# Filler constant first, no GpSimd copies, pad rows by DMA, and new engine lists in a fused attention and gated-MLP kernel

## The chip, the cores and the metric

The kernel runs on one core of a Trainium2 chip. A core has a matrix engine (TensorE, PE in the profile; PEld is its weight load), a vector engine (VectorE, DVE), a scalar engine with lookup tables (ScalarE, ACT), a general engine (GpSimd, POOL) and SyncE (SP), which here only issues DMAs. The engines run their own instruction streams in order and wait for one another through semaphores. Tensors live in SBUF (128 partitions); matmul results go to PSUM (eight banks), from which DVE or ACT must carry them away before a bank is used again. The metric is device time in microseconds, the median of several runs.

## What is computed

One layer with two halves, 2048 tokens, width 448, bfloat16. First a local attention: 16 heads of width 28, each token attends to itself and seven earlier tokens at a distance of 2, 4, ... 14. Then a gated MLP whose gate mixes all tokens with a 2048x2048 matrix.

```python
def A(x):                       # x is layernorm(input)
    qkv = x @ wqkv              # 448 -> 3 x 16 heads x 28
    idx = pos[:, None] - 2 * arange(8)[None, :]
    logits = einsum('bhsd,bhswd->bhsw', q, k[idx]) * 28 ** -0.5
    attn = softmax(where(idx >= 0, logits, -1e9))
    return einsum('bhsw,bhswd->bhsd', attn, v[idx]) @ wo
def B(x):                       # x is layernorm(h)
    z = gelu(x @ w_in)          # 448 -> 1792
    z1, z2 = z[..., :896], layernorm(z[..., 896:])
    g = einsum('ts,bsf->btf', w_sp, z2) + b_sp
    return (z1 * g) @ w_out     # 896 -> 448
h = x + A(layernorm(x)); out = h + B(layernorm(h))
```

## The kernel before

The kernel builds some 660 tasks, each a few instructions on one engine, and replays them in the order of five lists (`SEQ`: SP, POOL, DVE, ACT, PE, in that order), written out as task numbers. A planner class replays the lists with a cost for each task; this decides which PSUM banks and ring buffers a task gets, and how many filler matmuls go into a gap of PE. `Sched.issue` puts in the semaphore waits that the data needs. On the chip each engine then runs its list in order. `XV_ON` and the `alts` of a task say which engines may do it; the list in which its number stands decides.

The tokens are kept as 16 blocks of 128; unit u is the pair of blocks u and u+8. The work goes through these stages:

- Loads: x (`ld_x`, on SP and ACT), the q, k and v parts of `wqkv` (`ld_w` through `ld_rows`, lines 545 to 558, four DMAs each: two of 384 rows, two of 64 rows, alternating between the SP and ACT queues).
- First layernorm, unit by unit (`ln_unit`, line 616): statistics on DVE (line 622), aggregation on DVE (627), the reciprocal root on POOL (613, 614) or ACT (638, 639), normalization on DVE (646) into a ring, then a transpose into `xh`. Units 0 to 2 are transposed by PE and copied from PSUM (copies of every sort are on lines 608 and 610); units 3 to 7 by a DMA transpose on SP (653).
- The q and k weights are copied into a padded form, 32 columns to a head (`cpq`, `cpk`, on DVE or ACT), after GpSimd has zeroed the pads (593).
- q and k projections (line 764) in three chunks of tokens; two of 256 or 270 columns for each of k and q before the one of 512. The last chunk needs units 4 to 7.
- Nine attention tiles of 114 tokens. For each: a strided copy of `xh` into `xv` (`xv`, line 802; all nine on POOL), the v projection (812) and its evacuation (`evv`), logits (843), exp (857), a band mask on DVE (865), row sums (878), ln and exp for the reciprocal (887, 912), the product with v (901), and the scaling into `oT` (920).
- The output projection (958) and the residual sum on DVE (967) for each unit, then the second layernorm. The output weights `wo2` hold two heads in partitions 0 to 27 and 32 to 59; GpSimd first zeroes partitions 0 to 63 (`c_wo0`, line 597), two DMAs of 28x8 rows fill them, and `cpwo` (POOL) copies partitions 0 to 63 to 64 to 127.
- The MLP: `w_in` matmuls (979 and 1022) with gelu on ACT (989, 1032), a layernorm of z2 (995 to 1009), the token mixing (1056) from transposed loads of `w_sp` (939), gating on DVE (1066, 1073), the last projection (1082), the sum and the stores. The `w_sp` loads are chained: each waits until the one before it has landed.

PE, ACT and DVE share the four pairs of PSUM banks, so an evacuation that comes late holds a later matmul. The filler (`fill`, line 600) issues matmuls of 512 columns from a tile of ones, `warm`, which the task `c_warm` writes on DVE (line 586); the planner puts fillers only into gaps that begin after that task. In the list of before `c_warm` stands behind most of the first layernorm, and the built program holds no filler. The planner's price for a matmul does not depend on how long PE has been busy.

Of the kernel before, what the change touches and what calls it, by code (L numbers as in the profile page):

```python
# [6 lines left out]
D = 448  # L7
DH = 28
FH = 896
# [6 lines left out]
NC7 = 7  # L16
# [13 lines left out]
F32 = mybir.dt.float32  # L30
# [11 lines left out]
XV_ON = ("dve", "act", "pool")  # L42
# [184 lines left out]
class Planner:  # L227
# [64 lines left out]
    def replay(self, t0=0.7):  # L292
# [13 lines left out]
        for _ in tasks:  # L306
# [32 lines left out]
            dur = t.occ  # L339
            if e == "pe":  # L340
                live = [(f, s) for s, f in enumerate(self.pools["ps"]) if f is not None]
                if live and self.filler[0].end is not None:
                    tf, bank = min(live)
                    at = max(free[k], tf + 0.3, self.filler[0].end + 0.1)
                    if now - at > self.FILL[0]:
                        if pe_first is None:
                            pe_first = at
# [802 lines left out]
```

## Time and profile before

| | us |
|---|---|
| median of 3 runs | 252.19 (252.17 to 253.67) |
| the profiled execution | 250.46 |
| its span, first to last instruction | 248.7 |

The profile is of one execution. "Busy" counts instructions at work, without the issuing of DMAs; a DMA issue is shown on its queue (SPq, ACTq). The span in 40 slices of 6.2 us, the busy share of each in tenths:

```profile
PE   0699979969988999999999999999999999999995
DVE  4897725677999899078880002329010281553453
ACT  2639984667997556575850000000000000000000
POOL 6161630510083023014250000000000000000000
```

The first 13 or 14 slices are the attention and the start of the MLP, with work for all four engines; from the 14th on PE is full to the end. A row of the timeline gives start, duration, engine, line, operation, output and inputs with their shape, the count, and in brackets the idle time ahead of it with what ended it; rows of one kind that follow each other are merged, and the duration is that of the merged group. A row of the chain gives start, duration and what it was. A row of a group gives the count, the busy us, the mean ns of one, and the idle time ahead of it.

### The profile page before, as it was taken

The numbers are of one execution on the slowest core, as the hardware profiler recorded it, in microseconds if no ns is written. First come the engines' busy times: TensorE is split into PE (matmuls) and PEld (weight loads), VectorE is DVE, ScalarE is ACT, GpSimd is POOL, SyncE is SP. The second block draws the span as 40 slices with busy tenths as digits, with TensorE's granted clock in tenths as the row PEclk, the third lists the DMA queues.
The fourth block names the chain that finished last, engine by engine and source line by source line (L and its number), as shares of the span: only waits on it lengthen the run. The fifth ranks groups of instructions, "written<-read, shape, count | busy, mean of one in ns | idle before, by whom it ended". The sixth has DMA issues, their size and how long they took to land.

```text
span 248.7 us, 6335 instructions
## 1 busy us (share of the span) xinstructions
PE 231.4 (93%) x2822; PEld 121.3 (49%) x2822; DVE 136.4 (55%) x280; ACT 88.1 (35%) x104; POOL 40.7 (16%) x77
## 2 busy tenths in 40 slices
PE   0699979969988999999999999999999999999995
PEld 0476746445553555555544444444444444444552
DVE  4897725677999899078880002329010281553453
ACT  2639984667997556575850000000000000000000
POOL 6161630510083023014250000000000000000000
PEclk9999999999999999999999999999999999999999
DMA  6953698695349575677556333000000000000123
GB/s 184 349 154 64 165 148 191 124 179 106 44 26 206 101 194 60 133 161 134 130 87 168 85 87 84 0 0 0 3 0 0 0 3 0 0 0 18 58 101 122
DMA packets 56759, 22.81 MB, mean 92 GB/s; under 512 B 46668, under 2 KB 56604, under 8 KB 56732
## 3 DMA queue, kind: packets, MB, share of 16 engines
q1 hardware_dynamic: 55004, 20.98, 39.9%
q10 hardware_dynamic: 1728, 1.43, 1.8%
q8 instruction: 22, 0.36, 0.6%
q14 instruction: 5, 0.04, 0.0%
HBM read 9.20 MB, written 1.84 MB: 44 GB/s over the span
## 4 chain that ended last, share of the span: by engine, by line
PE 79%; DVE 11%; ACT 3%; DMA 2%; POOL 2%; ACTq 1%; issue 1%; DVEq 0%; POOLq 0%
PE psum L1056 39%; PE psum L979 9%; PE psum L1082 9%; PE psum L1022 9%; PE psum L764 7%; PE psum L958 4%; DVE reg L865 3%; DMA z2p<-in_A_wqkv_dram 2%; ACT reg L608 2%; DVE tring L646 2%; PE psum L812 2%; DVE st L622 2%; DVE x_tm L967 1%; DVE reg L610 1%; POOL rs L614 1%; PE psum L901 1%
## 5 line engine op out<-in xcount | busy, mean ns | idle before, releaser
L1066 DVE TENSOR_TENSOR reg<-psum,reg 128x512 bf16<-128x512 f32 x28 | 18.9, 687 | 69.9 <-PE psum L1056 69.8
L1056 PE MATMUL psum<-reg,z2p 128*128 128x512 bf16 x224 | 49.0, 379 | 0.0
L1056 PE MATMUL psum<-wspT_lo,z2p 128*128 128x512 bf16 x224 | 48.8, 379 | 0.0
L1056 PEld LDWEIGHTS psum<-wspT_lo,z2p 128*128 128x128 bf16 x224 | 21.9, 98 | 26.6 <-DVE z2p L1009 0.4
L1056 PEld LDWEIGHTS psum<-reg,z2p 128*128 128x128 bf16 x224 | 21.9, 98 | 26.3
L764 PE MATMUL psum<-xh,reg 64*128 64x256 bf16 (+2 forms) x336 | 28.9, 330 | 3.0 <-ACT reg L912 1.8
L608 ACT ACTIVATE reg<-psum 128x1024 bf16<-128x1024 f32 (+2 forms) x23 | 20.5, 917 | 9.9 <-PE psum L764 8.5
L764 PEld LDWEIGHTS psum<-xh,reg 64*128 64x128 bf16 x336 | 17.3, 103 | 12.4 <-ACT reg L608 2.2
L979 PE MATMUL psum<-w_in,xh 64*128 64x448 bf16 x224 | 22.6, 349 | 0.0
L1022 PE MATMUL psum<-xh,w_in 64*128 64x512 bf16 x196 | 22.2, 376 | 0.0
L995 DVE BATCH_NORM_STATS2 st<-z2p 128x6 f32<-128x448 bf16 x32 | 17.7, 608 | 8.2 <-ACT z2p L989 8.2
L1082 PE MATMUL psum<-reg 128*128 128x448 bf16 x112 | 21.7, 352 | 0.0
L622 DVE BATCH_NORM_STATS2 st<-x_tm 128x6 f32<-128x448 bf16 x32 | 18.9, 610 | 0.6 <-DMA x_tm<-in_A_x_dram 0.4
L989 ACT ACTIVATE z2p<-psum 128x896 bf16<-128x896 f32 x16 | 14.2, 917 | 8.7 <-PE psum L979 8.7
L1032 ACT ACTIVATE reg<-psum 128x1024 bf16<-128x1024 f32 x14 | 13.6, 1026 | 10.4 <-PE psum L1022 10.4
L857 ACT ACTIVATE reg<-psum 128x928 bf16<-128x928 f32 x18 | 16.1, 942 | 2.5 <-PE psum L843 2.5
L979 PEld LDWEIGHTS psum<-w_in,xh 64*128 64x128 bf16 x224 | 12.4, 94 | 9.3 <-issue 1.0
L614 POOL TENSOR_TENSOR rs<-rs,nhalf 128x2 f32<-128x2 f32 x19 | 16.1, 846 | 1.6
L1082 PEld LDWEIGHTS psum<-reg 128*128 128x128 bf16 x112 | 11.0, 98 | 10.4
L1022 PEld LDWEIGHTS psum<-xh,w_in 64*128 64x128 bf16 x196 | 11.0, 94 | 9.9 <-ACT reg L1032 0.5
L646 DVE TENSOR_SCALAR tring<-x_tm,mv,rs 128x448 bf16<-128x448 bf16 x32 | 14.6, 486 | 2.0 <-POOL rs L614 1.7
L865 DVE TENSOR_TENSOR reg<-reg,mband 128x928 bf16<-128x928 bf16 x18 | 13.5, 775 | 3.8 <-ACT reg L857 3.8
(63 smaller groups left out, 185.8 us busy)
## 6 DMA issues: line engine op xcount, KB each, us to landing
w_in<-in_B_w_in_dram SPq DMA_DIRECT2D x4, 672.0 KB, 5.3
out_dram<-tring SPq DMA_DIRECT2D x16, 112.0 KB, 1.7
x_tm<-in_A_x_dram SPq DMA_DIRECT2D x6, 224.0 KB, 6.0
reg<-in_B_w_out_dram SPq DMA_DIRECT2D x1, 784.0 KB, 4.5
z2p<-in_A_wqkv_dram ACTq DMA_DIRECT2D x2, 336.0 KB, 5.1
z2p<-in_A_wqkv_dram SPq DMA_DIRECT2D x2, 336.0 KB, 5.4
reg<-in_B_b_sp_dram SPq DMA_DIRECT2D x1, 512.0 KB, 4.1
w_in<-in_B_w_in_dram SPq DMA_DIRECT2D x4, 112.0 KB, 3.3
```

The lines of the kernel that those rows point to most:

```text
L608: iss("act", lambda e: e.activation(dst, src, AF.Copy), reads=rd, writes=wr)
L614: iss("pool", lambda e: e.tensor_tensor(dst, dst, nh, ALU.pow), reads=rr + [r_nhalf], writes=rr)
L622: iss("dve", lambda e: e.bn_stats(st[:, b, :], x_tm[:, b, :]), reads=[r_x[b]], writes=[rl[b]])
L646: iss("dve", lambda e: e.tensor_scalar(tring[:, h[0], :].rearrange("p (c s q f) -> p s q c f", c=NC7, s=2, q=2)[:, n], x_tm[:, b, :].rearr ...
L764: iss("pe", lambda e, k=k, s=s, gi=gi, lhs=lhs: e.matmul(psum[:, bk[s] * 512 + cw * gi:bk[s] * 512 + cw * gi + cw], lhs, xh[64 * s:64 * s ...
L865: iss(tk[0].eng, lambda e: e.tensor_tensor(ev, ev, mk, ALU.mult), reads=[r_E[es[0]][n], r_mband], writes=[r_E[es[0]][n]])
L979: iss("pe", lambda e, c=c, s=s: e.matmul(psum[:, zb[s] * 512:zb[s] * 512 + D], xh[64 * s:64 * s + 64, ROWS[s][c], HX + 128 * u:HX + 128 * ...
L995: iss("dve", lambda e, b=b: e.bn_stats(st3[:, b, k, :], z2p[:, b, D * k:D * k + D]), reads=[r_z2[b][k]], writes=[r_st3[b][k]])
L1022: iss("pe", lambda e, c=c, s=s: e.matmul(psum[:, bk[s] * 512:bk[s] * 512 + 512], w_in[64 * s:64 * s + 64, c, 128 * f:128 * f + 128], xh[64 ...
L1056: iss("pe", lambda e, b=b: e.matmul(psum[:, gb[0] * 512:gb[0] * 512 + 512], z2p[:, b, 128 * f:128 * f + 128], src[:, b, 512 * (tc % 2):512 ...
L1066: iss("dve", lambda e: e.tensor_tensor(ub[:, us_[0], :], psum[:, gb[0] * 512:gb[0] * 512 + 512], bb[:, 512 * tc:512 * tc + 512], ALU.add), ...
L1082: iss("pe", lambda e, f=f: e.matmul(psum[:, wb[0] * 512:wb[0] * 512 + D], z1p[f][:, 128 * m:128 * m + 128], w_out[:, f, :], start=(f == 0) ...
```

## The change

The diff does six things.

1. `c_warm` becomes the first task on DVE. All first statistics are made dependent on it, so that the lists keep it there.
2. `XV_ON` loses "pool", and `cpwo` stands on DVE: no copy is left on GpSimd.
3. The pads of the output weights are loaded instead of zeroed. `c_wo0` is gone. Each group of 28 rows is loaded as 32 rows, the next head's first four rows in the pad; the last group of the second half takes its pad from four earlier rows. (The matching rows of `oT` are zero, since V's pads are zero.) Four DMAs take the place of two.
4. The 64-row pieces of the q and k weights are loaded together: two DMAs of 64x2 rows for both in place of four. `ld_rows` is split into `rows384` and `rows64`.
5. In the planner, `COLD` takes the place of a fixed first stretch: after 1.8 us without a matmul, PE work counts up to 4.5 us as running at half speed.
6. All five lists are new. The first projections come later or earlier among the attention tiles, evacuations change between DVE and ACT, reciprocal roots between ACT and POOL.

```diff
-XV_ON = ("dve", "act", "pool")
+XV_ON = ("dve", "act")
...
-    FILL = (0.5, 0.25, 0.427, 0.216, 3.4)
+    FILL = (0.5, 0.25, 0.427, 0.216)
+    COLD = (1.8, 4.5)
...
+                if now - pe_end > self.COLD[0]:
+                    pe_run = now
+                cold = max(0.0, pe_run + self.COLD[1] - now)
+                dur += min(dur, 0.5 * cold)
                 dur += self.fetch(t.nmm, now, dur, True)
+                pe_end = now + dur
...
+        w_qk = z2flat[:, 0:2 * NC7 * D].rearrange("p (w c n) -> p w c n", w=2, c=NC7)
+        w_ld = {p: w_qk[:, n] for n, p in enumerate("qk")}
...
+        r_ld["k"][2:] = r_ld["q"][2:]
...
+        def rows384(name, dst, src, res, engs):
+            nb = 384 * src.shape[1] * 2
+            return [dma(engs[n], "%s%d" % (name, n), lambda e, d=d, f=f: e.dma_start(d, f.rearrange("(k p) n -> p k n", p=128)), nb,
+                        writes=[res[n]], issue=0.6) for n, (d, f) in enumerate(((dst[:, 0:3, :], src[0:384, :]), (dst[:, 3:6, :], src[64:448, :])))]
+
+        def rows64(name, dst, src, res, engs):
+            nb = 64 * src.shape[1] * 2
+            return [dma(engs[n], "%s%d" % (name, 2 + n), lambda e, d=d, f=f: e.dma_start(d, f), nb, writes=[res[2 + n]], issue=0.5, bw=180.0)
+                    for n, (d, f) in enumerate(((dst[0:64], src[384:448, :]), (dst[64:128], src[0:64, :])))]
...
-        c_wo0 = cst("c_wo0", [(lambda e: e.memset(reg3[0:64, 0:8 * D].bitcast(F32), 0.0), [], r_wo[0:2])], 1.55)
...
-                tb.append(add("bn%d_%d" % (which, b), "dve", 0.53, em, deps=[src_deps[n]]))
+                tb.append(add("bn%d_%d" % (which, b), "dve", 0.53, em, deps=[src_deps[n]] + ([c_warm] if which == 1 else [])))
...
-        for e_ in range(2):
-            t_wo.append(dma("sp", "wo%d" % e_, lambda e, e_=e_: e.dma_start(
-                wo2[32 * e_:32 * e_ + DH, :, :], A_wo.rearrange("(g h d) n -> h d g n", g=8, h=2)[e_]), DH * 8 * D * 2,
-                writes=[r_wo[e_]], deps=[c_wo0], bw=160.0))
+        for n, (dst, src) in enumerate((
+                (wo2[0:32], bass.AP(A_wo.tensor, A_wo.offset, [[D, 32], [2 * DH * D, 8], [1, D]])),
+                (wo2[32:64, 0:7], bass.AP(A_wo.tensor, A_wo.offset + DH * D, [[D, 32], [2 * DH * D, 7], [1, D]])),
+                (wo2[32:32 + DH, 7], A_wo[15 * DH:16 * DH, :]),
+                (wo2[32 + DH:64, 7], A_wo[15 * DH - 4:15 * DH, :]))):
+            t_wo.append(dma("sp", "wo%d" % n, lambda e, d=dst, f=src: e.dma_start(d, f), (256, 224, 28, 4)[n] * D * 2,
+                            writes=[r_wo[n]], bw=160.0))
...
-        tk.append(add("cpwo", "pool", 3.6, lambda: copy(tk[0].eng, wo2[64:128], wo2[0:64], r_wo[0:2], [r_wo[2]]), deps=t_wo,
-                      alts={"pool": 3.6, "dve": 1.10, "act": 3.15}))
+        tk.append(add("cpwo", "dve", 1.0, lambda: copy(tk[0].eng, wo2[64:128], wo2[0:64], r_wo[0:4], [r_wo[4]]), deps=t_wo,
+                      alts={"dve": 1.0, "act": 3.1}))
```

What the lists say around the start and the attention, by task names. `xv` number i belongs to tile i, `evv` is the evacuation of v, `evq` and `evk` those of q and k, `nrm` and `bn` belong to the layernorm, `cp` are weight copies, `ot` scales the product with v, `h` is the residual sum, `tD` a transpose by DMA, `wsp0` a load of `w_sp`, `wo` of the output weights, `win` of `w_in`.

| engine | before | after |
|---|---|---|
| PE, start | two transposes, halo transpose, 112 projection matmuls | 14 fillers, two transposes, halo transpose, 1 filler, 112 projection matmuls |
| ACT, loads | x8, x9, wk, wq, wk, wq, then the table load | x9, x8, wqk, the table load, then wq, wk, wv |
| DVE, weight copies | cpq0, cpk1 (cpq1 and cpk0 on ACT) | cpq0, cpq1, cpk1 (cpk0 on ACT) |
| xv | nine on POOL | 0, 1, 2, 3, 6, 7 on ACT; 4, 5, 8 on DVE |
| evv on DVE | 4 | 0, 3, 5 |
| q and k evacuations on DVE | evk2_0, evk2_1, evq2_1 | evq1_0, evk2_2, evq2_1 |
| first reciprocal roots on ACT | units 0, 1, 2, 5, 6 | units 0, 1, 6 |
| DVE around cpwo | (on POOL, between xv4 and xv6) | evk2_2, evq2_1, cpwo, xv4, ot3, h0 |
| SP in the middle | tD of unit 6, wsp0_0, wo1, wsp0_8, win, win, wo0, wsp0_1 | tD of unit 6, wsp0_0, wo2, win, wsp0_8, win, wsp0_1, wo1 |

More of the change, by code (lines that the diff above doesn't have):

```diff
@@ L303, in replay @@
         ptr, free = [0] * 5, [t0] * 5
-        loaded = pe_mode = pe_first = None
+        loaded = pe_mode = None
+        pe_end, pe_run = -9.0, 0.0
         dma_free = 0.0
@@ L353, in replay @@
                             nf += 1
+                            pe_end = x
                         if nf:
@@ L434, in bass_sequential_preLN__sliding_local_dilated__mixer_gmlp__prompt_kernel @@
         z2flat = z2p[:, :, :].rearrange("p b f -> p (b f)")
-        w_ld = {p: z2flat[:, NC7 * D * n:NC7 * D * n + NC7 * D].rearrange("p (c n) -> p c n", c=NC7) for n, p in enumerate("qk")}
+        w_qk = z2flat[:, 0:2 * NC7 * D].rearrange("p (w c n) -> p w c n", w=2, c=NC7)
+        w_ld = {p: w_qk[:, n] for n, p in enumerate("qk")}
         w_ld["v"] = wv
@@ L470, in bass_sequential_preLN__sliding_local_dilated__mixer_gmlp__prompt_kernel @@
         r_ld = {p: [Res("ld%s%d" % (p, s)) for s in range(4)] for p in "qkv"}
+        r_ld["k"][2:] = r_ld["q"][2:]
         r_w = {p: [Res("w%s%d" % (p, j)) for j in range(2)] for p in "qk"}
         r_xv = [Res("xv%d" % i) for i in range(NXV)]
-        r_wo = [Res("wo%d" % h) for h in range(3)]
+        r_wo = [Res("wo%d" % h) for h in range(5)]
         r_win = [[Res("w_in%d_%d" % (z, n)) for n in range(4)] for z in range(2)]
@@ L522, in dve_f32, with dma @@
             return (40.0 + 1.065 * n) / 1000.0
-        def dma(eng, name, fn, nbytes, deps=(), reads=(), writes=(), rel=(), store=False, issue=0.42, bw=340.0, setup=0.4, lead=1.5, after=()):
+        def dma(eng, name, fn, nbytes, deps=(), reads=(), writes=(), rel=(), store=False, issue=0.42, bw=350.0, setup=0.4, lead=1.5, after=()):
             def em():
@@ L543, in ld_x, with ld_wqk @@
                 t_x[b] = t
-        def ld_rows(name, dst, src, res, engs, issue):
-            w = src.shape[1] * 2
-            parts = ((dst[:, 0:3, :], src[0:384, :].rearrange("(k p) n -> p k n", p=128), 384, 0),
-                     (dst[:, 3:6, :], src[64:448, :].rearrange("(k p) n -> p k n", p=128), 384, 1),
-                     (dst[0:64, 6, :], src[384:448, :], 64, 2),
-                     (dst[64:128, 6, :], src[0:64, :], 64, 3))
-            return [dma(engs[n % len(engs)], "%s%d" % (name, n), lambda e, d=d, f=f: e.dma_start(d, f), rows * w,
-                        writes=[res[k]], issue=issue if rows > 64 else 0.42) for n, (d, f, rows, k) in enumerate(parts)]
+        def rows384(name, dst, src, res, engs):
[6 more added lines that the diff above has]
+                    for n, (d, f) in enumerate(((dst[0:64], src[384:448, :]), (dst[64:128], src[0:64, :])))]
         t_w = {}
+        SPACT = ("sp", "act")
         def ld_w(p):
             c0 = "qkv".index(p) * D
-            t_w[p] = ld_rows("w" + p, w_ld[p], A_wqkv[:, c0:c0 + D], r_ld[p], ("sp", "act"), 0.6)
+            t_w[p] = rows384("w" + p, w_ld[p], A_wqkv[:, c0:c0 + D], r_ld[p], SPACT)
+        def ld_wqk():
+            t = rows64("wqk", w_qk[:, :, 6, :], A_wqkv[:, 0:2 * D], r_ld["q"], SPACT)
+            t_w["q"] = t_w["q"] + t
+            t_w["k"] = t_w["k"] + t
         t_win = {}
```

17 lines of the change are left out of this document (10 added, 7 removed), and 59 rows, old and new, of the table SEQ.

## The prediction

> **What bounds the kernel now.** I read the page's busy shares first, then a table of stages (start and end of the stretch, its length, then busy us and instruction count of PE, PEld, DVE, ACT and POOL, granted clock, DMA share, GB/s).
>
> ```profile
> PE 231.4 (93%) x2822; PEld 121.3 (49%) x2822; DVE 136.4 (55%) x280; ACT 88.1 (35%) x104; POOL 40.7 (16%) x77
> 24.00:36.00 12.00, 10.67 (x304) 7.55 (x300) 7.10 (x19) 11.32 (x17) 6.04 (x13) 1.00 0.84 149
> 36.00:48.00 12.00, 11.45 (x228) 6.21 (x230) 5.94 (x4) 6.56 (x8) 2.68 (x1) 1.00 0.81 169
> 48.00:60.00 12.00, 9.59 (x308) 5.37 (x306) 9.04 (x11) 8.13 (x9) 1.44 (x2) 1.00 0.79 145
> 60.00:82.00 22.00, 20.62 (x716) 11.73 (x712) 21.03 (x41) 19.21 (x23) 7.80 (x10) 1.00 0.54 94
> 82.00:100.00 18.00, 18.00 (x186) 9.84 (x186) 16.56 (x37) 10.28 (x11) 3.97 (x8) 1.00 0.62 118
> ```
>
> From 82 us on PE never stops: 18.00 of 18.00, and the chain of waits is PE alone from there to 245.8. The change alters the order of that part but not its number of matmuls, so it keeps its length, and the whole question is how much earlier PE gets there. Ahead of 82 the bound changes: ACT from 24 to 36 (11.32 of 12), DVE from 60 to 82 (21.03 of 22). PE lost 12.00-10.67, 12.00-11.45, 12.00-9.59 and 22.00-20.62, 5.7 us in all, between 24 and 82.
>
> Next, the start, from the timeline of PE, two stretches of line 764 alone, and the chain:
>
> ```profile
> 0.79 0.40 SPq L572 DMA_DIRECT2D z2p<-in_A_x_dram  x1
> 10.57 9.13 PE L764 MATMUL psum<-xh,reg 64*128 64x256 bf16 x112 [1.18 <-DVE xh L610]
> 19.63 0.56 PE L662 MATMUL psum<-ident,tring 128*128 128x128 bf16 x7
> 26.78 1.70 PE L764 MATMUL psum<-xh,reg 64*128 64x256 bf16 x28
> 28.32 1.49 PE L812 MATMUL psum<-reg,xv 64*128 64x448 bf16 x14
> 10.57:13.57 3.00, 3.00 (x30) 1.00 1.10 355
> 13.57:16.57 3.00, 3.00 (x32) 1.00 0.63 187
> 16.57:19.57 3.00, 3.00 (x58) 1.00 0.06 13
> 29.73 0.17 DVE L586 MEMSET warm<- 128x128 bf16 x1
> 3.56 5.69 DMA z2p<-in_A_wqkv_dram
> 9.37 0.63 DVE reg L610
> 9.99 0.54 DVE xh L610
> 127.82 72.63 PE psum L1056 x336
> ```
>
> The first 112 projection matmuls take 10.57 to 19.63, 9.06 us. The same shape later takes 26.78 to 28.32 for 28, 1.54 us, so 6.16 for 112. The stretches show where it goes: about 30 matmuls in each of the first two 3 us, 58 in the third. PE runs at half rate for some 6 us, until about 16.5, though the granted clock reads 1.00 throughout. That costs 9.06-6.16 = 2.9 us. The constant for the filler matmuls is written at 29.73, and no filler runs at all.
>
> **The change part by part.**
>
> *Filler first.* The constant (0.17 us) goes to the head of DVE, and 14 fillers of 512 columns stand on PE before the first transpose, one more before the first projection. A warm 512-column matmul takes 72.63/336 = 0.216 us, so a cold one 0.432, and 14 cold ones 6.05 us: from about 1.1 (SP starts at 0.79; DVE has nothing to wait for either, and writes the constant) to 7.1. PE had no work there until the first normalized block was transposed, at 7.44 in the row below, so idle time covers them, with some 0.3 us over.
>
> ```profile
> 7.44 1.67 PE L662 MATMUL psum<-ident,tring 128*128 128x128 bf16 x14 [7.44 <-DVE tring L646]
> ```
>
> The fillers last about as long as the half rate did (10.57 to 16.5, 5.9 us), so the projections should find PE at full rate: gain 2.9. The bounds are 0 (still cold) and 2.9. I take 2.9. [...]
>
> *First loads.* The chain ran through the last small piece of the q weights, landing at 9.24 behind all of the k weights, then through two DVE copies to 10.57.
>
> ```profile
> 4.10 1.28 ACT L513 ACT_TABLE_LOAD   x1 [4.10 <-issue]
> z2p<-in_A_wqkv_dram ACTq DMA_DIRECT2D x2, 336.0 KB, 5.1
> 9.35 1.51 ACT L608 ACTIVATE reg<-z2p 128x1568 bf16<-128x1568 bf16 x1
> L610 DVE COPY reg<-z2p 128x1568 bf16<-128x1568 bf16 x2 | 1.2, 618 | 1.0 <-DMA z2p<-in_A_wqkv_dram 1.0
> ```
>
> Now the last q piece is one of 336 KB on the ACT queue, ahead of k and v, but behind the table load (1.28) and three other issues (0.40 for the first in SP's row, some 0.5 for these larger ones) from 0.8 on: issued near 3.6; with 5.1 us to landing it is there at 8.7. DVE also makes the xh copy before the weight copy instead of after it. Then the weight copy ends between 9.3 and 10.05 (landing as late as 9.24), against 10.53. Gain 0.5 to 1.2, or 0 if the table load delays the piece further; I take 1.0. Against it: the second half of the q weights (1.51 on ACT at 9.35) moves to DVE behind two statistics (0.6 each), a small copy (0.2) and its own 0.62, 2.0 us after the first half, while the first q block occupies PE for 1.54. A new wait of 0.5. So PE should finish the 112 matmuls 2.9+1.0-0.5 = 3.4 us earlier, near 16.2.
>
> *GpSimd copies.* These rows (timeline) show what a GpSimd copy or long memset does to DVE beside it:
>
> ```profile
> 13.70 0.67 DVE L646 TENSOR_SCALAR tring<-x_tm,mv,rs 128x448 bf16<-128x448 bf16 x2
> 16.02 1.59 POOL L597 MEMSET reg<- 64x1792 f32 x1
> 16.14 1.90 DVE L646 TENSOR_SCALAR tring<-x_tm,mv,rs 128x448 bf16<-128x448 bf16 x2
> 45.32 3.17 POOL L610 COPY reg<-reg 64x3584 bf16<-64x3584 bf16 x1 [9.52 <-DMA reg<-in_A_wo_dram]
> 45.60 3.94 DVE L865 TENSOR_TENSOR reg<-reg,mband 128x928 bf16<-128x928 bf16 x2 [3.79 <-ACT reg L857]
> 50.59 1.18 DVE L865 TENSOR_TENSOR reg<-reg,mband 128x928 bf16<-128x928 bf16 x2
> 51.27 0.39 PE L878 MATMUL psum<-reg,ones 64*32 64x464 bf16 x8 [1.82 <-DVE reg L865]
> ```
>
> Two normalizations take 0.67 alone and 1.90 beside the memset; two masks take 1.18 alone and 3.94 beside the copy of the output weights, ending 1.05 after it. PE then waited 1.82 us for a mask. Prices for what moves, from the groups:
>
> ```profile
> L610 POOL COPY xv<-xh 128x896 bf16<-128x896 bf16 x9 | 8.4, 938 | 14.3 <-PE psum L812 6.4 <-DVE xh L702 5.1 <-DMA xh<-tring 2.4
> L608 ACT ACTIVATE reg<-psum 128x896 bf16<-128x896 f32 x8 | 7.3, 916 | 1.3 <-PE psum L812 1.2
> L610 DVE CAST reg<-psum 128x896 bf16<-128x896 f32 x1 | 1.1, 1076 | 0.0
> ```
>
> Six of the nine xv copies go to ACT, nearest row 0.92 each; three to DVE, no row, between 0.62 (the weight copy) and 1.08 (the cast); I take 1.0, since its source is strided. The output weights' copy on DVE has half the partitions and 3584/1568 of the elements of the 0.62 row: at most 1.4, I take 1.1.
>
> *To 36 us.* ACT takes four xv copies (3.7) and one xh copy (0.9); it gives away a weight copy (1.5), two v evacuations (1.8), one q evacuation (about 1.0) and two reciprocal roots: even at most, so ACT, the bound there, can hold the lead. DVE gets the weight copy (0.6), those two v and one q evacuations (3x1.1), and gives up an xh copy (0.6) and 1.2 of port wait at 16 us: some 2 us more, in a stretch where it is busy 7.10 of 12. What released PE's next stage:
>
> ```profile
> 28.16 4.64 SPq L653 DMA_TRANSPOSE xh<-tring  x3
> 30.86 0.70 DVE L646 TENSOR_SCALAR tring<-x_tm,mv,rs 128x448 bf16<-128x448 bf16 x2
> 36.55 4.00 PE L764 MATMUL psum<-xh,reg 64*128 64x512 bf16 x42 [1.82 <-ACT reg L912]
> ```
>
> The ACT instruction named writes nothing that these matmuls read; they need all of xh, whose last normalizations end at 31.56 and whose last transpose is issued right after. Those normalizations come as much earlier as DVE allows, between 0.5 (the earlier first statistics alone) and 3.4 (the whole lead). I take 2.7: a loss of 0.7 from the lead.
>
> *36 to 60 us.* The mask delay (3.94-1.18 = 2.8 on DVE, 1.8 on PE) goes. DVE gets the weight copy and two xv, 3.1, into stretches where it is busy 5.94 and 9.04 of 12. Gain between 1.8 and -1; I take 1.3.
>
> ```profile
> 70.85 0.89 DVE L646 TENSOR_SCALAR tring<-x_tm,mv,rs 128x448 bf16<-128x448 bf16 x1
> ```
>
> *60 to 82 us.* DVE, the bound, gets one xv (1.0) and one v evacuation (1.08) and loses about 0.5 of port wait (0.89 in the row above against 0.67/2): +1.6, of which the 0.97 idle can take a part: +0.6 (0 to +1.6). ACT's extra 0.9 fits in its 2.8 idle. The rest I cost at nothing. The GpSimd constants in a new order are covered by the idle of that engine (busy 6.04 and 2.68 of 12 us from 24 to 48); should one of them come late, the q weight copy would wait for it, us for us. The pad rows are 64 more rows of 896 bytes, 57 KB.
>
> Sum: -2.9-1.0+0.5+0.7-1.3+0.6 = -3.4. The profiled execution took 250.46 (span 248.7), so 247.1 there; the median of the runs is 252.19, 1.7 above it, so the median goes to 248.8.
>
> **The rivals.** *The lead is swallowed* (0.22): the last normalizations come only 0.5 earlier because DVE now carries weight copies and evacuations among them. For it: DVE's order is full of foreign work there; against: the port waits go. 0.5+1.3-0.6 = 1.2 gained: 251.0.
>
> *The clock opens late* (0.10): the 2.9 is lost, 251.7. For it: the fillers last only as long as the half rate did. [...]
>
> *More goes* (0.13): 2.5 of the 5.7 us that PE lost between 24 and 82 go beyond the terms above: 246.3.
>
> *Slower* (0.10): the copy of the output weights now stands on DVE ahead of an xv copy, the scaling of tile 3 and the first residual sum, and waits for the last big piece of those weights, which SP issues behind three chained w_sp loads instead of two.
>
> ```profile
> 40.32 0.57 SPq L926 DMA_DIRECT2D reg<-in_A_wo_dram  x1
> 41.15 6.08 SPq L939 DMA_TRANSPOSE wspT_lo<-in_B_w_sp_dram  x2
> ```
>
> Each link takes some 3.0 (6.08/2) us. Before, the last piece was issued at 40.32 and read at 45.32; now one link later but 2.7 earlier, so there near 45.6, while DVE should reach the copy near 46. Every us that it lands later holds DVE, and PE behind it. It eats the whole gain at 49.4 and makes the kernel over 1% slower past 51.9; at 52.1, 254.9. For it: no slack; against: it needs two more links.
>
> That the fillers don't run is no case: they stand first in the built order.
>
> **How the numbers follow.** One per cent, about what a measurement here can tell, is 2.5 us: faster is below 249.7. The forecast has 0.45; with "more goes", faster 0.58. The two rivals at 251.0 and 251.7 make "same" 0.32, the last one slower 0.10. Leaving out the slower case and the outer half of "more goes", the range is 245.9 to 251.7.
>
> **What would show it.** Right: a filler group from about 1 us; line 784 (764 before) with 112 matmuls in 6.2 us from about 9.6; the 512-column projections starting near 34; no DVE mask pair above 1.3 us; PE unbroken from about 78.5. Wrong: half rate after 10 us; the last xh transposes still issued at 31; a DVE wait on the output weights; DVE past 82 with PE waiting for residual sums.

## The result, and the profile after

| | median | lowest to highest | runs |
|---|---|---|---|
| before | 252.17 us | 250.34 to 253.67 | 7 |
| after | 249.18 us | 248.39 to 250.62 | 7 |

The ratio is 0.9898, with a 95% interval of 0.9854 to 0.9943: 3.0 us faster, where 3.4 were forecast (249.18 against 248.8). Whether it is more than one per cent the interval leaves open. The ratios and intervals here and below leave out executions more than 1.5 per cent longer than the shortest of the same kernel, and the medians count all.

The two profiled executions don't show this difference: 250.46 before, 250.62 after. Before's is shorter than six of the seven runs of its median, after's is the longest of its seven. The mean granted clock of each execution explains part of it. It is 1.000 in the profile of before and 0.986 in that of after, which shows two stretches of 3.4 us at half rate (14 to 17.4 and 75.5 to 79, below). One such stretch lowers the mean by 3.4/2/249 = 0.0068 and costs up to 1.7 us, so 0.993 is one and 0.986 two. Of 68 executions of the kernel before that stood beside the experiments, 57 had one, 7 none and 4 two; of the seven of the changed kernel two had one and five two. The 57 average 252.5 us and the seven without a stretch 251.6. So some 0.9 of the offset of 1.7 us that the prediction carried from profile to median goes with one half-rate stretch, and the changed kernel has more of them. What the rest is isn't shown; the projections began early in the profile of before (10.57, below).

The profile after, first the busy shares, then the same table of stages as before:

```profile
PE 236.0 (95%) x2837; PEld 118.9 (48%) x2837; DVE 137.0 (55%) x286; ACT 89.6 (36%) x104; POOL 27.5 (11%) x70
```

```profile
24.00:36.00 12.00, 11.40 (x256) 7.87 (x258) 8.58 (x18) 11.19 (x17) 1.87 (x6) 1.00 0.63 107
36.00:48.00 12.00, 11.84 (x288) 6.05 (x286) 4.82 (x7) 9.82 (x11) 0.00 (x0) 1.00 0.77 155
48.00:60.00 12.00, 11.42 (x348) 6.46 (x344) 11.25 (x13) 8.44 (x10) 0.00 (x0) 1.00 0.76 189
60.00:82.00 22.00, 18.77 (x636) 10.40 (x633) 17.68 (x36) 17.49 (x21) 3.49 (x6) 0.92 0.51 86
82.00:100.00 18.00, 18.00 (x221) 8.98 (x215) 16.95 (x38) 10.35 (x12) 4.17 (x11) 1.00 0.82 134
```

From 24 to 60 PE is idle for 1.3 us, where it was 4.3. From 60 to 82 it is idle for 3.2 us, where it was 1.4, and the clock there is 0.92. DVE, the bound of that stage before, has 4.3 us to spare. From 82 on PE is busy without a break in both. The timeline of the start:

```profile
1.10 4.51 PE L622 MATMUL psum<-warm 128*128 128x512 bf16 x14 [1.10 <-DVE warm L607]
9.64 1.70 PE L784 MATMUL psum<-xh,reg 64*128 64x256 bf16 x28 [1.13 <-DVE reg L630]
10.57 0.63 DVE L642 BATCH_NORM_STATS2 st<-x_tm 128x6 f32<-128x448 bf16 x1 [0.99 <-DMA x_tm<-in_A_x_dram]
12.02 0.63 DVE L642 BATCH_NORM_STATS2 st<-x_tm 128x6 f32<-128x448 bf16 x1 [0.82 <-DMA x_tm<-in_A_x_dram]
12.68 0.62 DVE L630 COPY reg<-z2p 128x1568 bf16<-128x1568 bf16 x1
13.35 6.42 PE L784 MATMUL psum<-xh,reg 64*128 64x256 bf16 x84 [2.01 <-DVE reg L630]
19.71 0.51 PE L682 MATMUL psum<-ident,tring 128*128 128x128 bf16 x6
```

The first 28 projection matmuls run from 9.64 at full rate (1.70). Then PE waits 2.01 us for the second half of the q weight copy. That copy (12.68) stands on DVE behind two statistics of unit 2, each of which waits for a load of x. The 84 matmuls behind it take 6.42 us, where 84 at full rate take 4.76 (a row of after_order, below), and the 112 end at 19.71, as before (19.63). The windows of one microsecond, with the granted clock third from the end, show the half rate; the last three are from the later stage:

```profile
13.00:14.00 1.00, 0.65 (x12) 0.59 (x14) 1.00 (x5) 0.38 (x1) 0.39 (x2) 1.00 1.10 316
14.00:15.00 1.00, 1.00 (x14) 0.70 (x12) 0.88 (x3) 1.00 (x1) 0.88 (x3) 0.53 1.09 353
16.00:17.00 1.00, 1.00 (x14) 0.67 (x12) 0.09 (x2) 1.00 (x2) 0.86 (x3) 0.50 0.23 72
...
73.00:74.00 1.00, 0.00 (x0) 0.00 (x0) 1.00 (x2) 0.57 (x1) 0.00 (x0) 1.00 0.54 112
76.00:77.00 1.00, 1.00 (x12) 0.12 (x8) 0.25 (x1) 0.40 (x1) 0.00 (x0) 0.50 0.91 296
78.00:79.00 1.00, 1.00 (x10) 0.39 (x8) 1.00 (x3) 0.25 (x1) 0.00 (x0) 0.55 0.11 43
```

Behind the idle 2.0 us the clock was at half rate again, from 14 to 17.4. It is not so in every execution: after_pool and after_order, below, waited 2.12 and 2.16 us in the same place and kept the full rate. The later stages, on the timeline:

```profile
35.59 1.69 PE L784 MATMUL psum<-xh,reg 64*128 64x512 bf16 x14 [0.56 <-issue]
46.47 1.19 DVE L885 TENSOR_TENSOR reg<-reg,mband 128x928 bf16<-128x928 bf16 x2 [4.96 <-ACT reg L877]
49.99 1.09 DVE L630 COPY reg<-reg 64x3584 bf16<-64x3584 bf16 x1
65.99 0.28 PE L921 MATMUL psum<-reg 64*32 64x58 bf16 x22 [1.41 <-issue]
74.26 0.29 PE L863 MATMUL psum<-reg 28*64 28x58 bf16 x11 [1.52 <-issue]
74.48 2.23 PE L981 MATMUL psum<-reg 64*128 64x448 bf16 x16
```

The mask pair takes 1.19 where the copy on GpSimd had stretched it to 3.94. The copy of the output weights (49.99) waits for nothing. What took the lead back are the two rows with "issue": PE stopped for 1.41 and 1.52 us, in the middle of a run of small matmuls, while nothing that the profile shows was missing. After the second the clock is at half rate from 75.5 to 79 (2.23 us for 16 matmuls that take 1.69 elsewhere).

### The profile page after: what moved, and what is told of

Same layout as the page of the kernel before. It is cut to its first block, busy times and chain, and to the rows that moved or that the text cites. A ratio compares the mean times of both kernels' runs of the same rounds, so it can differ in the third digit from the quotient of the medians.

```text
span 248.9 us, 6345 instructions
## 1 busy us (share of the span) xinstructions
PE 236.0 (95%) x2837; PEld 118.9 (48%) x2837; DVE 137.0 (55%) x286; ACT 89.6 (36%) x104; POOL 27.5 (11%) x70
## 4 chain that ended last, share of the span: by engine, by line
PE 88%; DMA 3%; DVE 3%; issue 2%; SPq 1%; ACT 1%
PE psum L1079 39%; PE psum L784 10%; PE psum L1002 9%; PE psum L1105 9%; PE psum L1045 8%; PE psum L832 5%; PE psum L981 4%; DMA x_tm<-in_A_x_dram 3%; PE psum L921 2%; PE psum L863 2%; DVE x_tm L990 1%; PE psum L898 1%; ACT reg L628 1%; DVE reg L885 1%; SPq L550 1%
## 5 line engine op out<-in xcount | busy, mean ns | idle before, releaser
L784 PE MATMUL psum<-xh,reg 64*128 64x256 bf16 (+2 forms) x336 | 27.4, 320 | 4.0 <-DVE reg L630 3.1
L784 PEld LDWEIGHTS psum<-xh,reg 64*128 64x128 bf16 x336 | 16.5, 99 | 13.8 <-DVE reg L630 3.7
L1002 PE MATMUL psum<-w_in,xh 64*128 64x448 bf16 x224 | 22.0, 349 | 0.0
L628 ACT ACTIVATE reg<-psum 128x1024 bf16<-128x1024 f32 (+2 forms) x21 | 19.1, 917 | 7.5 <-PE psum L784 4.7
L1045 PE MATMUL psum<-xh,w_in 64*128 64x512 bf16 x196 | 21.6, 376 | 0.0
L633 POOL TENSOR_SCALAR rs<-mv 128x2 f32<-128x2 f32 x21 | 6.1, 292 | 96.6 <-DVE mv L647 77.9
L885 DVE TENSOR_TENSOR reg<-reg,mband 128x928 bf16<-128x928 bf16 x18 | 11.1, 634 | 8.6 <-ACT reg L877 8.6
L1002 PEld LDWEIGHTS psum<-w_in,xh 64*128 64x128 bf16 x224 | 10.7, 94 | 10.3 <-issue 0.2
L634 POOL TENSOR_TENSOR rs<-rs,nhalf 128x2 f32<-128x2 f32 x21 | 15.3, 729 | 1.7
L1045 PEld LDWEIGHTS psum<-xh,w_in 64*128 64x128 bf16 x196 | 9.5, 94 | 11.5
```

The costliest lines, as they stand in the source:

```text
L628: iss("act", lambda e: e.activation(dst, src, AF.Copy), reads=rd, writes=wr)
L634: iss("pool", lambda e: e.tensor_tensor(dst, dst, nh, ALU.pow), reads=rr + [r_nhalf], writes=rr)
L784: iss("pe", lambda e, k=k, s=s, gi=gi, lhs=lhs: e.matmul(psum[:, bk[s] * 512 + cw * gi:bk[s] * 512 + cw * gi + cw], lhs, xh[64 * s:64 * s ...
L1002: iss("pe", lambda e, c=c, s=s: e.matmul(psum[:, zb[s] * 512:zb[s] * 512 + D], xh[64 * s:64 * s + 64, ROWS[s][c], HX + 128 * u:HX + 128 * ...
L1045: iss("pe", lambda e, c=c, s=s: e.matmul(psum[:, bk[s] * 512:bk[s] * 512 + 512], w_in[64 * s:64 * s + 64, c, 128 * f:128 * f + 128], xh[64 ...
```

## The experiments

Edits are shown on the lists, by task names. All ratios are to the kernel before, on the same chip.

**1. The fillers.** In the first run the kernel before gets the constant as DVE's first task; with that its planner puts 17 fillers ahead of the transposes. In the second the changed kernel is built without its 15 fillers.

```diff
 before, DVE list
+c_warm bnh bn1_8 bn1_0 ...
-... nrm1_4 nrm1_12 c_warm mask0_0 ...
+... nrm1_4 nrm1_12 mask0_0 ...
 after, fill()
-            for _ in range(n):
+            for _ in range(0):
```

> The kernel before with one list entry moved: the filler constant first on DVE, so that 17 fillers stand ahead of the first transpose; nothing else changes. Theory A (the clock follows stretches of 3.4 us, as the profile after shows: granted 0.5 from 13.95 to 17.4 after a stretch in which PE stood idle for 2.0 us): the fillers open the clock near 4 us, PE then waits for the first q weights until 10.5, and either stays at full rate (112 projection matmuls in 6.2 us, end near 16.8) or falls back for one stretch (end near 18.4). Time 1.0 to 2.5 us below before. Rival B (the fillers bring nothing in a whole run, because ACT and DVE hold the attention): within 0.5 us of before.

Measured: 254.95, ratio 1.0091 (1.0058 to 1.0124), slower. From its timeline:

```profile
1.11 6.07 PE L604 MATMUL psum<-warm 128*128 128x512 bf16 x17 [1.11 <-DVE warm L588]
12.21 7.95 PE L766 MATMUL psum<-xh,reg 64*128 64x256 bf16 x112 [2.69 <-DVE xh L612]
```

> The changed kernel without its 15 fillers, all else as it is. Theory A: since PE falls back to half rate at 13.95 us anyway, the fillers give little to the changed kernel: the first 28 projection matmuls take 3.0 in place of 1.5 us, but the next 84 wait for DVE until 13.3 in both; the 112 end between 19.5 and 21, and the time is within 0.7 us of the changed kernel (248.5 to 250). Rival C (the fillers bring the 2.9 us that I forecast): about 252. Beside it: PE's instruction stream is 30 instructions shorter, so if the two pauses of PE without a releaser (64.6 and 72.7 us) are instruction fetches, they move to 15 matmuls earlier or later in the list, or change their length.

Measured: 249.46, ratio 0.9884 (0.9827 to 0.994), not told apart from the kernel with its fillers.

```profile
9.41 3.02 PE L785 MATMUL psum<-xh,reg 64*128 64x256 bf16 x28 [0.82 <-DVE reg L631]
12.60 5.06 PE L785 MATMUL psum<-xh,reg 64*128 64x256 bf16 x84 [0.16 <-DVE reg L631]
```

The fillers alone gain nothing, and in the kernel before they cost time, which neither theory had. There, PE waits 2.69 us behind them for weights and the copy that follows, and the projections run at half rate after all: 11 of 12 executions had two or three half-rate stretches (mean clock 0.980 or 0.987). In the changed kernel the cold matmuls, 3.02 us for 28, fill the time in which PE would wait for the second q copy (0.16 in place of 2.01), and the 112 end at 17.59, ahead of the profile with fillers.

**2. What the 112 wait for.** The second q copy ahead of the statistics of unit 2; then also the k weights' load ahead of the x loads.

```diff
 after, DVE list (both)
-... cpq0 bn1_2 bn1_10 evh cpq1 ag1_2 ...
+... cpq0 cpq1 evh bn1_2 bn1_10 ag1_2 ...
 after, SP list (the second only)
-... wqk2 x2 x10 wk0 x4 ...
+... wqk2 wk0 x2 x10 x4 ...
```

> The changed kernel with two DVE entries moved: the second q weight copy and the small halo copy stand ahead of the two statistics that wait for x. Theory A: the wait of 2.0 us ahead of the second projection block goes, and with it the half rate after it; but the third block then waits for the k weight copy on ACT, which had its weights at 13.6 us, so the 112 matmuls end near 18.2 and not near 16.2: 1.0 to 1.5 us below the changed kernel. Rival D (the DVE wait is the whole loss at the start): they end near 16.3, 2.5 to 3.4 us below. Rival E (whatever is won here is lost behind ACT and DVE by 82 us): no change within 0.5 us.

Measured: 248.55, ratio 0.9839 (0.9785 to 0.9892).

```profile
9.80 3.23 PE L785 MATMUL psum<-xh,reg 64*128 64x256 bf16 x56 [1.28 <-DVE reg L631]
14.81 3.23 PE L785 MATMUL psum<-xh,reg 64*128 64x256 bf16 x56 [1.78 <-ACT reg L629]
```

> The changed kernel with the second half of the q weight copy (and the halo copy) on DVE ahead of the statistics of unit 2, as in the run after_cpq1, and with the last k piece that GpSimd's queue-mate SP issues, wk0 (336 KB), ahead of x2 and x10 instead of behind them. Theory A (the 112 projection matmuls wait in turn for the weight copies; the copy that comes last is now cpk0 on ACT, which waits for wk0): the wait of 1.78 us ahead of the second 56 matmuls falls below 0.8, the 112 end near 17.0 instead of 17.98, and the median is 0.5 to 1 us under after_cpq1, about 247.8. Rival (the lead is swallowed by the transposes of the last units, whose x loads now land later): the 112 end earlier, but the 512-column projections start at 33.9 or later, and the median stays at 248.5 to 249.

Measured: 249.36, ratio 0.9886 (0.9844 to 0.9929).

```profile
10.04 4.76 PE L785 MATMUL psum<-xh,reg 64*128 64x256 bf16 x84 [1.47 <-DVE reg L631]
16.68 1.70 PE L785 MATMUL psum<-xh,reg 64*128 64x256 bf16 x28 [1.88 <-DVE reg L631]
```

The wait moves and stays: 2.01 us for the second q copy, then 1.78 for the first k copy, then 1.88 for the second k copy, which now stands behind the delayed x loads. The 112 end at 17.98 and 18.32, and the second run is far from the 247.8 expected. So it seems to be the loads as a whole that hold this place, not one copy; the median of the first is below the changed kernel's, but their intervals overlap.

**3. The copy of the output weights.** Before with this copy on DVE, and nothing else; and after with it on GpSimd.

```diff
 before, POOL and DVE lists
-POOL: ... xv5 xv4 cpwo xv6 ...
+POOL: ... xv5 xv4 xv6 ...
-DVE: ... mask2_0 evv4 ot3 ...
+DVE: ... mask2_0 evv4 cpwo ot3 ...
 after, DVE and POOL lists
-DVE: ... evk2_2 evq2_1 cpwo xv4 ...
+DVE: ... evk2_2 evq2_1 xv4 ...
-POOL: ... c_kpad rs2_0 ...
+POOL: ... c_kpad cpwo rs2_0 ...
```

> The kernel before with one entry moved: the copy of the output weights on DVE, behind the fourth v evacuation, in place of GpSimd. Theory F (the GpSimd copy held DVE by the port): no mask pair above 1.3 us, the PE pause of 1.8 us at 49.5 shrinks to under 0.8, and the time falls by 0.7 to 1.8 us. Rival G (DVE is the bound from 60 to 82 us, so the extra 1.1 us on it gives the gain back): within 0.5 us of before.

Measured: 250.50, ratio 0.9914 (0.9875 to 0.9953): this one move is worth 2.1 us, the size of the mask delay (2.8 on DVE, 1.8 on PE). It is not the clock: executions with one half-rate stretch average 250.6, those of the kernel before beside them 252.5. Its stretch from 48 to 60, and the masks that were held before:

```profile
48.00:60.00 12.00, 11.70 (x328) 6.21 (x324) 9.36 (x11) 8.71 (x11) 0.94 (x1) 1.00 0.63 139
```

```profile
48.29 1.19 DVE L867 TENSOR_TENSOR reg<-reg,mband 128x928 bf16<-128x928 bf16 x2 [3.79 <-ACT reg L859]
```

> The changed kernel with the copy of the output weights back on GpSimd, nothing else moved. If the port wait of DVE beside a GpSimd copy is what the move was worth: a GpSimd copy of about 3.2 us somewhere from 44 to 52, a DVE instruction beside it that takes over 2 us where it took 1.2 or less, and a median 1 to 3 us above the changed kernel, 250 to 252. Rival (the gain of that move came from the order of the lists around it, not from the engine): the DVE instruction is held, but PE does not wait longer than before, and the median stays within 0.7 of 249.2.

Measured: 249.57, ratio 0.987 (0.9821 to 0.992), no difference from the changed kernel that these runs resolve.

```profile
43.59 3.17 POOL L631 COPY reg<-reg 64x3584 bf16<-64x3584 bf16 x1 [18.11 <-DMA reg<-in_A_wo_dram]
44.88 2.92 DVE L886 TENSOR_TENSOR reg<-reg,mband 128x928 bf16<-128x928 bf16 x2 [4.89 <-ACT reg L878]
50.13 0.39 PE L899 MATMUL psum<-reg,ones 64*32 64x464 bf16 x8 [0.82 <-DVE reg L631]
```

DVE is held just as before, 2.92 for 1.19, but 43.6 to 46.8 is a place where DVE had been idle for 4.89 us and PE was in 70 projections of 512 columns, until 49.0. Behind them PE waits 0.82 us for DVE, which it does not in the changed kernel. In these two places the price of the GpSimd copy was that of the DVE work beside it. (The profile is of the longest of the six executions, 252.23.)

**4. The pauses.** They stand at fixed counts of matmuls in PE's own stream. One pause at 516 or 531 stands in all kernels of the changed lists ahead of the first 512-column projections, moves with the fillers, and is left out. The others, over 0.25 us and up to the mixing, from the timelines of PE:

| kernel | pauses at matmul number (us) |
|---|---|
| before | 1493 (0.32), 1621 (0.63) |
| before_filler | 1621 (1.45) |
| before_cpwo | 1494 (0.50), 1622 (1.41) |
| after | 1114 (0.30), 1369 (1.41), 1624 (1.52) |
| after_nofill | 731 (0.43), 986 (1.50), 1369 (1.59), 1624 (0.46) |
| after_cpq1 | 730 (0.28), 1368 (1.94) |
| after_wk0 | 1368 (1.70) |
| after_pool | 985 (1.62), 1368 (2.03), 1624 (0.27) |

The numbers lie about 128 or 255 apart. Without the 15 fillers the same numbers fall 15 matmuls later in the work, and the pauses are still at 986, 1369 and 1624. The profile of either kernel lists a DMA queue "instruction" of 22 packets and 0.36 MB, 16 KB each, and 2837 matmuls with as many weight loads are some 258 instructions to a packet. So by the counts PE waits there for the next block of its program. The times of that queue's packets in the traces say the same: in the changed kernel two of them end at 64.70 and 72.67, and PE goes on at 65.99 and 74.26, 1.3 and 1.6 us later. Each of the 18 pauses of the table, and of six more in the runs below, ends 0.9 to 1.6 us behind the end of a packet. Ahead of number 1369 of the changed kernel 146 small matmuls run in 2.2 us (62.38 to 64.57). Most crossings of such a boundary are hidden here, but up to four in an execution cost 0.3 to 2.0 us each (the table).

Two ideas of what makes a block late were tried: DMA transposes in its way (three loads of `w_sp` moved out of the stretch, alone and with experiment 2), and too little matmul time ahead of the boundary (two groups of 16 wide matmuls moved into that time).

```diff
 after_wsp and after_wk0_wsp, SP list
-... win0_3 wsp0_4 tD2_0 wsp0_12 win0_0 tD2_1 wsp0_5 ... tD2_6 wsp0_13 ...
+... win0_3 tD2_0 win0_0 tD2_1 ... tD2_6 wsp0_4 wsp0_12 wsp0_5 wsp0_13 ...
 after_order and after_cpq1_order, PE list
-... mmo4_0 mmr4 mmy1 mmr5 mmo4_1 mml8_0 ... mmo8_1 mml7_0 mml7_1 mmy4 ...
+... mmo4_0 mmr4 mmr5 mmo4_1 mmy1 mml8_0 ... mmo8_1 mmy4 mml7_0 mml7_1 ...
 after_cpq1_order, PE list
-... mmq2_2 mmo3_0 ...
+... mmo3_0 mmq2_2 ...
```

> The changed kernel with three of the chained w_sp loads (blocks 4, 12 and 5 of the first half, issued at 62.20, 71.76 and 82.21) moved on SP behind the last transpose of the second layernorm. Theory B (PE's two pauses of 1.41 and 1.52 us with no releaser, at 64.6 and 72.7, are waits for PE's own instructions, which are fetched by DMA, some 255 matmuls at a time, and come late behind a DMA transpose): the pause at about 64.6 shrinks below 0.5, the one at 72.7 below 1.0 (a transpose of xh still stands there), the half rate after 75 goes, and the median falls by 2 to 4 us to 245.5 to 247. Rival (the pauses have another cause, or the fetch is late by itself): both pauses stay above 1 us, and the median stays at 249.

Measured: 251.21, ratio 0.9939 (0.9909 to 0.9969), 2.0 above the changed kernel by the medians, with intervals that overlap. The pauses, a window inside the first, and what the move cost later:

```profile
64.21 0.28 PE L922 MATMUL psum<-reg 64*32 64x58 bf16 x22 [1.14 <-issue]
72.22 0.29 PE L864 MATMUL psum<-reg 28*64 28x58 bf16 x11 [1.26 <-issue]
126.45 2.54 PE L623 MATMUL psum<-warm 128*128 128x512 bf16 x11
```

```profile
63.00:64.00 1.00, 0.07 (x9) 0.00 (x0) 1.00 (x5) 0.95 (x2) 0.42 (x2) 1.00 0.00 0
```

No transfer runs beside the block here: its packet goes from 61.86 to 62.84, the last one before it ends at 61.59, and none follows up to the end of the pause. The pause is still 1.14, so the transposes are not its cause, and the packet takes as long alone (0.98) as beside them in the changed kernel (0.95). Whether they add the 0.27 that the pause there is longer, one profile of each can't tell. And the loads now come so late that the planner filled the start of the mixing with 11 fillers, 2.5 us. They may be what the median lost, but the profiled execution has them too and took 249.28, so this is not shown.

> Both edits of after_wk0 and of after_wsp in one kernel. If theories A and B hold and do not overlap, about 1.4 us (A) and 2 to 4 us (B) below the changed kernel: 244 to 246. If both only move the same half-rate stretch, it is no better than the better one of the two.

Measured: 252.15, ratio 0.9974 (0.994 to 1.0008); the same 11 fillers, a pause of 1.66 at 1368, and far from the 244 to 246 expected.

> The changed kernel with two output-projection groups (16 matmuls of 448 columns, 1.69 us each) moved on PE, nothing else: the one of unit 1 from ahead of the last product of tile 4 to behind it, the one of unit 4 from behind the logits of tile 7 to ahead of them. In every profile so far PE's pauses without a releaser stand at the same counts of matmuls in its own stream (1368 or 1369, 1624; also 730 and 985, about 127.7 or a multiple of it apart), with and without fillers ahead and with and without transposes beside them. Theory B2 (a block of PE's instructions is asked for a fixed number of instructions before it is needed, and takes 3 to 4 us to come; if the matmuls in between are all small ones, they are through before it is there): each of the two intervals now holds 1.69 us more of matmul, so the pause at 1368 falls from 1.41 to below 0.4 and the one at 1624 from 1.52 to below 0.4, wherever these counts now fall, no half rate follows in 75 to 79, and the median falls by 1.5 to 3 us, to 246.5 to 247.7. Rival (the pauses belong to the matmuls there, or to something else on the chip at that time): a pause of over 1 us stays, at other counts, and the median stays within 0.7 of 249.2.

Measured: 247.25, ratio 0.9777 (0.9741 to 0.9813). The interval lies below that of the changed kernel, but it rests on four of the six executions, those without a half-rate stretch, whose mean is 247.0. With the other two (250.17 and 250.22, two stretches and one) the mean is 248.1, against 249.4 of the changed kernel, and the intervals would overlap. There is no pause at 1368 or 1624, nor at any other block, and from 60 to 82 PE is busy 19.94 us at full clock, where it was 18.77 at 0.92.

```profile
60.00:82.00 22.00, 19.94 (x654) 11.64 (x656) 19.61 (x38) 19.49 (x23) 4.56 (x8) 1.00 0.59 110
```

```profile
13.51 4.76 PE L785 MATMUL psum<-xh,reg 64*128 64x256 bf16 x84 [2.16 <-DVE reg L631]
73.81 0.39 PE L899 MATMUL psum<-reg,ones 64*32 64x464 bf16 x8 [1.42 <-DVE x_tm L991]
```

> The two moves of after_order and the DVE order of after_cpq1 in one kernel, with one projection group (q, 14 matmuls of 512 columns, 1.69 us) of the third chunk moved on PE to behind the first product of tile 3, which puts it into the interval ahead of count 985. By theory B2 no pause without a releaser above 0.5 us at 985, 1368 or 1624, and the median 1.5 to 3 us below after_cpq1: 245.5 to 247. By the rival it is like after_cpq1, 248.5.

Measured: 248.09, ratio 0.9805 (0.9758 to 0.9853): no pause either, and above the 247 expected; three of its executions had one half-rate stretch, the other three lie at 247.0 to 247.3, as in after_order. The earlier q copy adds nothing to it.

In after_order the packets of the two blocks end at 62.31 and 70.14, 1.6 and 2.0 us before PE is at 1369 (63.93) and 1624 (72.16): with the moved groups the blocks are there in time. The other executions bear it out: of the four kernels with these moves (two of them in part 5) 15 of 24 had no half-rate stretch, of the seven kernels with the changed lists and without the moves 5 of 55.

So here a run of small matmuls used up a block before the next one was there. It is not the whole rule. In those seven kernels the last 128 matmuls ahead of 1369 took 1.9 to 2.0 us and a pause came in all; ahead of 1624 they took 2.1 to 2.2, and it came in four. In after_pool 4.1 us stood ahead of 985, and the pause of 1.62 came all the same, because the packet began late, at 52.30, 0.9 us before the pause. What decides when a block is asked for stays open, and no run shows theory B2's fixed lead or its 3 to 4 us: the packets of the changed kernel take 0.88 to 1.42 us. In after_order's rows above the 84 projections keep the full rate behind their wait of 2.16, and the longest wait from 60 to 82 is now one for DVE, 1.42 for a residual sum.

**5. Two more edits of after_order:** no fillers; and five of the nine xv copies back on GpSimd.

```diff
 order_nofill: after_order, and in fill()
-            for _ in range(n):
+            for _ in range(0):
 order_xvpool: after_order, DVE, ACT and POOL lists
-DVE: ... xv5 ... xv4 ... xv8 ...   ACT: ... xv7 ... xv6 ...
+POOL: ... c_kpad xv5 xv4 xv7 xv8 rs2_0 xv6 rs2_1 ...
```

> The kernel of after_order with no filler matmuls emitted. Theory C (what the fillers gain in the first 28 projection matmuls, 3.0 against 1.7 us, is spent as a wait for the second half of the q weight copy, whose time is set by x loads and DVE): the first 28 take about 3 us from 9.4 to 9.7, the wait behind them falls from 2.16 to below 0.9, the 112 end at 17.5 to 18.5 as with fillers (18.2), and the median is 246.6 to 247.9. Rival (fillers also keep the clock from falling during that wait, so that without them one more half-rate stretch comes): a median of 248.5 to 249.5.

Measured: 250.12, ratio 0.9869 (0.9805 to 0.9932), outside what theory C gave.

```profile
9.75 3.17 PE L785 MATMUL psum<-xh,reg 64*128 64x256 bf16 x28 [1.21 <-DVE reg L631]
13.26 5.37 PE L785 MATMUL psum<-xh,reg 64*128 64x256 bf16 x84 [0.34 <-DVE reg L631]
53.93 0.67 PE L864 MATMUL psum<-reg 28*64 28x58 bf16 x58 [1.17 <-issue]
```

The start went as theory C has it (wait 0.34, the 112 end at 18.6). But a pause of 1.17 came up at 986, where after_nofill too had one (1.50) and the kernels with fillers mostly none: every boundary falls 15 matmuls later in the work. By the median the rival's 248.5 to 249.5 was missed as well. Its six executions go from 247.87 to 252.79, three of them without a half-rate stretch (mean 248.7). Its interval just touches that of after_order, so the price of leaving out the fillers there, and how much of it is the shift, stays open.

> The kernel of after_order with the last five xv copies (tiles 4 to 8; three from DVE, two from ACT) on GpSimd, as in the kernel before; the first four stay on ACT. Theory D (a GpSimd copy holds DVE, but from 45 to 80 us PE seldom waits for DVE, as the run with the output weights' copy on GpSimd showed): DVE gets about 3 us of work less and some normalizations or masks of 1.9 instead of 0.7 to 1.2 us beside the copies; the median stays within 0.8 of after_order, 246.5 to 248.0. Rival (the price of a copy on GpSimd is what the change removed): DVE late at the masks or residual sums, PE waits of over 1 us in 50 to 80, and a median of 248.5 or more.

Measured: 248.76, ratio 0.9847 (0.9792 to 0.9902): 1.5 above after_order, with intervals that overlap. The median is the rival's (248.5 or more), but its sign is missing: no wait of PE between 50 and 80 is over 1 us, the longest is 0.88. Its pair of masks beside a GpSimd copy took 1.90 us:

```profile
67.53 1.90 DVE L886 TENSOR_TENSOR reg<-reg,mband 128x928 bf16<-128x928 bf16 x2
67.86 1.07 POOL L631 COPY xv<-xh 128x896 bf16<-128x896 bf16 x1 [1.15 <-PE psum L833]
```

Two pauses of 0.49 (at 1369) and 0.55 (at 1749) appeared too, so the price of the copies alone isn't settled.

## Why the prediction was right, and where its steps were wrong

The number was right by luck: few terms of the sum hold, and the errors of the others cancel.

- *Filler first*, -2.9: the clock did open in time, and the first 28 matmuls ran at full rate from 9.64, as forecast (9.6). But the 112 ended at 19.71 in this profile and at 18.1 to 18.2 in after_pool and after_order, whose clock held; not at 16.2. The step that failed is the next one, *a new wait of 0.5* for the second q copy: it measured 2.0 to 2.2 us, and 1.7 more (6.42 against 4.76) where the clock closed in it. I had counted the busy time of the two statistics ahead of the copy, 0.6 each, and not that each waits for a load of x, which now takes longer (median 8.1 us from issue to landing, 6.0 before). That gain and wait cancel, after_nofill shows (249.46 against 249.18); order_nofill leaves it open.
- *First loads*, -1.0: 10.57 to 9.64 in the two profiles. Three profiles with the old order of loads began at 10.57, 12.21 and 13.41, eleven with the new one between 9.41 and 10.62, so before's profile was a good case, and the new order may be worth more than the term: on these means (12.06 and 9.9) some 2 us, though no run moves the loads alone.
- *To 36 us*, a loss of 0.7: none. There was no lead at 19.7 to lose from, and 1.0 us of it at the 512-column projections: PE began them at 35.59, before at 36.55, and in after_pool, after_order and after_wsp at 34.1 to 34.6, which is where the prediction put them.
- *36 to 60*, -1.3: right in kind and too small. PE's idle time there fell from 2.96 to 0.74 us, 2.2, and one move, the copy of the output weights, was worth 2.1 by itself in the kernel before. That the copy on GpSimd delays the masks holds for its place there (the pair took 3.94 us beside it, 1.19 without); in the new order the pair took 2.92 beside it, at no price that the median shows (249.57 against 249.18). The rows show that DVE is held, not that a port does it, as the prediction and theory F name it.
- *60 to 82*, +0.6, DVE being the bound: wrong. DVE had 4.3 us to spare there. PE lost 2.9 us to two waits for its program and 1.7 to the half rate after them. The profile of before had the sign of it, two such pauses of 0.32 and 0.63, which I read as nothing. No term of the sum stood for such pauses.

Of the rivals, "slower" did not come about: the copy of the output weights waited for no load. "The lead is swallowed" named the wrong place: the lead was there at 52 (the first output projection at 51.79, before at 56.45, with 1.9 us of other work put behind it) and went at 64 and 73. "The clock opens late" did not happen in this form; it opened at about 4 us and closed again. "More goes" did not: PE was idle 4.6 us from 24 to 82, before 5.7. The lower end of the range, 245.9, was worked out from no row.

The 5.9 us at half rate in the trace before, which the prediction set the fillers against, are not what the clock takes to open each time: with the fillers it took 3.0 to 4.9 (below). But what the fillers were worth was spent on the wait.

## What to carry to other kernels

In this kernel small matmuls were a load on the program's own supply (146 in 2.2 us, then a pause of 1.41): where PE runs through some 150 of them without a wide one, look for rows whose idle time ends in "issue", count their place in the stream and compare it with the ends of the instruction queue's packets. Two wide groups moved ahead of two such boundaries took the pauses away and 1.9 us off the median (249.18 to 247.25), where the whole change had given 3.0. When an engine is to copy what another engine waits for, cost the instructions ahead of the copy by when their inputs land, not by their length. And before a profiled execution is compared with medians, compare its granted clock and its first DMA-bound start with those of other executions.

## What the hardware showed that I had not expected

- The clock can close after idle time that is shorter than the half-rate stretch that follows, 3.4 us: 2.0 us idle (11.3 to 13.35) were followed by 0.50 from 14 to 17.4, and the 1.52 us at 73 (with 1.41 at 65) by 0.50 from 75.5 to 79. It does not close each time: waits of 2.16 and 2.12 us at 13.5 in after_order and after_pool, and pauses of 1.14 and 1.26 in after_wsp and of 1.17 in order_nofill, were followed by no such stretch.
- The clock opens after a time that varies: 14 fillers took 4.51 us in one profile, which is 7 at 0.432 and 7 at 0.216, so it opened some 3.0 us behind the first; in after_wsp they took 5.45, which is 11 and 3, so 4.8 us. Over the nine profiles with 14 fillers (4.51 to 5.45 us) it is 3.0 to 4.9; the kernel before ran its first projections at half rate for some 5.9 us. In that first cold stretch the tables give the granted clock as 1.00 (before, 10.57 to 16.57, with half the matmul rate of the next 3 us); only later ones show (0.50).
- A block of PE's program can come 2 us late (1.94 at number 1368 in after_cpq1, 2.03 in after_pool). PE goes on only 0.9 to 1.6 us after its packet has landed: in after_wsp it stood for 1.14 us with no transfer running, the block having landed at 62.84, before the pause began (63.07).
